# Forgetting attention followed by a SwiGLU block: the normalization multiply of batches 2 to 7 on GpSimd, a bank for each half of the last product, and a new written-out order

## The chip, the cores and the metric

The kernel runs on one core of a Trainium2 chip. The time is that of one execution on the device, in microseconds (us). The kernel before took 356.89 us (median of 3 runs, 356.67 to 357.1). The engines are TensorE (PE, with its weight loads as PEld), VectorE (DVE), ScalarE (ACT), GpSimd (POOL) and SyncE (SP, which here only issues DMAs). Each engine works through its own instructions in the order in which they were issued, and waits on semaphores for the others.

## What is computed

Eight batches, eight heads, 576 positions, heads of 64. Attention with a learned decay, causal, then a root-mean-square normalization over the 512 columns of all heads, and a SwiGLU block of width 1536:

```python
scores = scale * np.matmul(q, k.transpose(0, 1, 3, 2))
cum = np.cumsum(np.log(np.clip(f, 0.0001, 1.0)), axis=-1)
decay = cum[:, :, :, None] - cum[:, :, None, :]
scores = np.where(causal, -1e9, scores + decay)
attn = softmax(scores)                       # over the last axis
x = np.matmul(attn, v)                       # to (B * S, H * D) = (4608, 512)
xn = x / np.sqrt(np.mean(x * x, axis=-1, keepdims=True) + 1e-06) * rms_g
g = xn @ w_gate                              # 512 x 1536
silu = g * (1.0 / (1.0 + np.exp(-g)))
out = (silu * (xn @ w_val)) @ w_out          # 1536 x 512
```

## The kernel before

**Tiling.** A batch has five chunks of rows, j = 0 to 4: four of 128 rows and one of 64. The chunks 0 to 3 of batch b are the 512 tokens of group g = b of the second part; the eight 64-row chunks together are group 8. For each batch the kernel loads q, k and v by chunk (L334, L346 and L357), turns q and k so that the head dimension lies on the partitions, forms blocks of scores on PE (L527), takes their exponential on ACT from PSUM to the tile `PT` or, for the smallest block, `P` (L546), zeroes the upper triangle of the blocks on the diagonal on POOL ("mask", L554), multiplies by the decayed v (L575) and divides by the row sum on DVE, which gives a chunk of `x` (L594, L598).

**Turning q and k.** The chunks 0 to 3 of batches 0 and 1 are turned by PE (`turn_pe`, L452, L458). Chunk 4 of those batches and everything of batches 2 to 7 is turned by a transposing DMA that SP issues (`turn`, L437); SP waits for the load of that chunk and then issues, strictly in its own order. The loads of q and k are DMAs that POOL issues (L334), one instruction of POOL each.

**The normalization** (`norm`, L607 to L661) takes one or two chunks at a time. ACT squares x and sums along the row (L623). POOL divides by 512, adds the small constant (L628) and raises to the power -0.5 (L629): this is the root `rs`. Then x is multiplied by `rs` to the bf16 tile `xn` (L637): DVE does it for chunks 0 and 1 of batch 0, ACT for the other 38. Of those 38, 30 belong to batches 2 to 7 (24 of 128 rows and 6 of 64). `xn` is turned by PE for the groups 0 and 1 and by a transposing DMA from SP (L659) for the others. The tile `x` has 6 buffers, `xn` has 4.

**The second part.** `gate` (L832) forms the gate and value products of a group; ACT takes a tanh (L844), DVE two products (L846, L839). `seven` (L767 to L818) does a part of the groups 5 to 8 with seven half-size products in place of eight, with copies on ACT, sums on DVE and a product on POOL (L818). `project` (L862 to L972) multiplies by `w_out`, also with seven products for eight: four sums of SBUF tiles on DVE first (L885, L888, L891, L894, 128x1536), then the products (L910), their copies (L917) and sums (L920) to `ores`, and the stores (L938, L940).

**The end.** In group 8 the last two products of `project` are halved by columns (`halved`): f4 takes the second half of one product (`w22`), f5 that of the other (`wt4`). PE does them in the order wt4 half 0, w22 half 0, wt4 half 1, w22 half 1. DVE adds each half to `ores` (L920, 128x256), and each half is stored in two pieces: one issued by SP, one by ACT.

**Order.** Nothing of the order is left to a scheduler. `Plan.add` collects 1964 units of work (an instruction or a few, a DMA, a wait), `ORDER` gives each a rank of two characters, `SLOTS` gives each of 1303 uses of a buffer its buffer, and the units are issued by rank. `0.72`, `0.45` and the like in the calls of `act`, `dve` and `pool` are durations for the search that made the strings; they have no effect on what runs.

Of the kernel before, what the change touches and what calls it, by code (L numbers as in the profile page):

```python
# [30 lines left out]
SEVEN = {5: (2,), 6: (0, 1, 2), 7: (0, 1, 2), 8: (0, 1, 2)}  # L31
# [9 lines left out]
    "gWk2k3kikjkQkRlplqksktkIkJm9mamcmdkXkYmBmC0F0N0H0L0G0R0V120O0U0v0E110Z1c151h1y1i1l1q1s1u1B13181j1z1k"
    "1A1K1E1Q211U221D1P0W102h1L3a262i2t2d242c1G1O3N2r2J2T2D2R342X3g2C2I1V254L3d3h3u444c4B4H40414v4w454P5a"
    "534i4j4a4b5c5h5p5s5l5D5N5K5O5u5v4V4W6j6R55565P5Q6T686p6z6h5G5H65667B6L6W767g7t7H7A7X6v6w6Y6Z8u7N807V"
    "8i8w8q8z6N6O7D7E708D8J8O81827T7U9q5S8W9799919k7K7L77789u9b9n9h9C8E8F8s8t8Q9x9P9D8L8Mahaibca3a8agaeas"
    "aVaGanaoazaAbGb9bfbubmc9cjcgckbEbFbpbqcycEbwbxaPaQdpcxcDcKcJbLbMc5c6dUcWd7dyd1dldxdqdCcLcMcXcYeCdFdR"
    "dXe1efe7ecdudvekelf0eAeMfadmdnexeydYcPfhfpftfsfJeFeGeXeYejfLfOfUfYfnfoePeQgdg6gggcdGdHfvfwgKgpgvh8gz"
    "gOgXh9gkglgegfghhhhphvhthKihhXiRgLgMhFhGhBgIhPhQhxhyiziEiWj2iJhahbieifhSj5jgjnjajrjAjvjCiBiCjIjJkcjT"
    "kbk4kqkGkzkDjpjqk8k9likPkWl6klkmjRjSlBkylmlulzlylKilimjxjyl8lJlTlXm5kSkTlVlWmrm6mgmbldlelDlEmZmpmymE"
    "mumFmLmMmvmwm1m2mNmUn0n6n8nhnknonF191b1a1f1o1r1p1C1J1M1T1Z2b2g2j2n2M2O3j3o3y3E3G3K4u4z4y4C5e5m5n5E5F"
    "5X6c6k7a7d7m7o7C7I85888e8p8m8v8N8R93969s9y9A9E9U9Ya2a4a7aaaBaFb7babJbObPbVczcIcVd2dodte0e6e5e9ebeieq"  # L50
    "evf7fbfffqfFfMg3gugmgrgZh3h4hAhmhshzhUhEhRhTi0j3j8jejhjojtjzjDjHjQkLkZl3l7loltlAlOlPlUlZm4mnmtmIn1mO"
    "mYn7nanfninCnHnTnXo2ou1g1t1x1X271F1N1W20232a2f2q2u2E2y2K2V2Z387lalb0d4d53B3V3Z484E4I4o4G4Y5Y646a6l6P"
    "746A6U726EmTndqWqX868f8l9d9i9j8A8Y8Z8S9a9e9r9v9w9z9F9GbWeTfgi2i3aSajaWbbbgbhbHbSbTbBbYc2cacecfcpcucv"
    "enfygthnhodIepeweZf4f5eUfHfIf6fAfCfRfVfWfKg0g1gTlflrlvlwhgisiwiAiZj0iPiTiUidi5ijiFjijjj4j6j7khl2monb"
    "ncjXjUk6lGlMlNkCl0l1lQmkmmmHn3n4mRmVmWnxnBnVo0o1mDngovp7papbpxpBpCofoJoOoZpvpwpPpTpUphpoqJr4r52m2x2v"
    "2B2L2e2H2s2w2Y2N2U2S2W333f3t3l3q3z4K3p3F433L3O694s323U393H423A3I3J3Q3S373k3e3i3v3M3X3T3W4d3R4Q584F5C"
    "4X5r5y4n504x4D5f3P4g3Y4h4p4A4S4O4Z59494J4k4t4R717b6x5g6Q7x6K755q6i5U6g6q57735d5i7h7i7Y7r7u8d7J877P7Z"
    "8j616t6d6u6S5k5L5x5z5T7c7y7s7z7F7S8B8k8y8K8X9f94989m8r8P8G909c7n7G7M7O7W8x8I8C8H8VbNcibRc4coa9apamar"
    "ayaJaUaRaZb4afaYaqatbibrbUbybIbZb3bvb8bebDclcOctcwd3axaOaDaTaXbXcccdchcAcqd0cNcUdfbdc3bsbQcbakaEauaC"
    "aMgigsgqgwgydre8dAdEedeVfrf3f8fBd6dwdcdsdBeteReBeJeWdzdJdMdTdVf9fZflfug7fmfNfQfSgbemeKeueEeSeDf2eLf1"  # L60
    "fkh7huhlhqhDdSeedZe2eoigiQioiuiXgxgSgFgYh5jLjVjWk0kahWiti8ikiKhCi9hJhLiihMi4hVi1iah0hrh6hchwjfjujmjw"
    "jGjljNjsjKk5k7kvknkpkBiyj9iSiYjkgJhdgPgUhklxlYmSnmd8kdn5nJnGlRnlnSmJnvnDnrnunKnNnRnEnYo4o7ogntnAnQnZ"
    "nLnIo3oiobohomoxnOnUojoFosoAoaolm8nnmlmxnsk1l5kwkElcmQoDn2neoPkolbkrkxlhnjnynqnznPkFmzkOllmGlFmflLmh"
    "mjlgm0lnlCm7nMocoporpnpHq4qbpLpQpVqjqdqhqzqopIq5pEpMqqq7qaq0qmqpqnqFpYqvqrqIqGqKquqwnWo5onozokotoCoN"
    "oIoLpzoSo6owoqoRoBoGoMoVp0p6oYp8oooEoWpepXq1p9pfoyoHoXp5oQoKoTpJpgplpNpAp1pdpcptpipspKpGpOpRpZq6p3py"
    "pFq8qEqTqcqDqtqLqPqxqyqBqOqUqQqVqZqYr9rfr1rmrdrnqArersrqrtrurBrNrxs4r8rzrrs7rvrAs8t9qiqlr6rhqCr0r3rk"
    "rbrCrJrKr2raroryrgrirprGrIrMrPrVqMrjrSsbsUsYrWs1s3s5rOses9scsispsnsqstsurErHrXs2s0rRsas6smsBslsJshsv"
    "sKsOswsAszsHsfsysDsksrsCsssIsGsQsTsNsXt5t0tqsjsPsLtjtksVsZtntgtotrtxsMtmtvtBt8tAtatttltEtethtKtMtOtP"
    "tRuatSuBtNtQtYuqubtVu6uwupuvuIuLtWuEuGuQucuKuuuAsEsStityt1tptstItUtXtLu1tutCu0u5tHtFtTu8u2u7ufurtctJ"
    "u3uFuhumulux545M5J6X5o6b5t6y5b5j5w5I8b8c5R676m6F6B6McGcH6V79aHaI959H9N9O929M9gaN9l9t9B9Ldgdh9K9Z9Vad"  # L70
# [86 lines left out]
def fox_ffn_kernel(ctx, tc, q, k, v, f, moe_w_gate, moe_w_val, moe_w_out, moe_rms_g, out):  # L157
# [449 lines left out]
    def norm(b, js, key):  # L607
# [23 lines left out]
        for i, j in enumerate(js):  # L631
# [3 lines left out]
            def emit(i=i, n=n, hx=hx, hn=hn):  # L635
                mul = nc.vector.tensor_scalar_mul if on_dve else nc.scalar.mul
                mul(T_xn[hn.slot][0:n, :], T_x[hx.slot][0:n, :], rs[:, i:i + 1])  # L637
# [426 lines left out]
```

## Time and profile before

| | |
|---|---|
| time, median of 3 runs | 356.89 us |
| the profiled execution | 359.89 us |
| its span, first to last instruction | 358.2 us |
| mean granted TensorE clock | 0.992 |
| instructions | 10502 |

The profile is of one execution, 3.0 us above the median of the runs; 1.7 us of its time lie around the span. A page of the profile gives the busy time of each engine and a list of the costliest groups of instructions. A group is written as line, engine, operation, tile written and tiles read, shape, count; then its busy time in us and the mean of one in ns; then how long the engine stood idle before them and who ended that. A window gives the busy time of each engine between two moments, with the number of instructions, the clock that TensorE was granted (1.00 is full speed) and the traffic. The chain of work that ended last is followed back from the last instruction; its pieces are given as start, length and what. SPq and ACTq are issues of DMAs by those engines.

### The profile page before, as it was taken

What the parts mean: (1) busy time and instruction counts of PE and PEld (TensorE: products, weight loads), DVE (VectorE), ACT (ScalarE), POOL (GpSimd) and SP (SyncE); (2) the same over time, 40 slices, a digit from 0 to 9 for tenths busy, and PEclk for the clock granted to TensorE, in tenths of its full rate; (3) what the DMA queues carried; (4) which work ended last, traced back from release to release, by engine and by line L of the source; (5) the groups of instructions that cost most, each with busy time, mean ns of one, the idle gap of its engine ahead of it and who ended that gap; (6) DMA issues with size and microseconds to landing.
All of it is one profiled execution on the core that took longest, in us unless ns stands there. A gap on an engine that the chain in (4) does not pass through costs nothing.

```text
span 358.2 us, 10502 instructions
## 1 busy us (share of the span) xinstructions
PE 337.3 (94%) x4272; PEld 263.1 (73%) x4298; DVE 277.6 (78%) x508; ACT 265.1 (74%) x441; POOL 206.4 (58%) x249
## 2 busy tenths in 40 slices
PE   1889997999999999999999999999999999999995
PEld 1669997878886556556756657757888888888884
DVE  3688988598677777778768879898886787758684
ACT  5679997897986867787786877888988575676510
POOL 8989762399468659685768637744142161243410
PEclk9999999899999999999999999999999999999998
DMA  9999999999959999999999969951014110110324
GB/s 134 201 166 185 214 154 146 117 180 117 199 111 140 173 141 174 168 163 139 141 161 182 162 123 181 191 97 38 9 59 104 46 44 3 60 59 2 121 93 112
DMA packets 161544, 44.88 MB, mean 125 GB/s; under 512 B 147092, under 2 KB 160920, under 8 KB 161496
## 3 DMA queue, kind: packets, MB, share of 16 engines
q0 software_dynamic: 76240, 16.26, 57.9%
q1 hardware_dynamic: 84648, 27.43, 41.0%
q8 instruction: 33, 0.54, 0.7%
q10 hardware_dynamic: 608, 0.52, 0.5%
q14 instruction: 15, 0.12, 0.1%
HBM read 37.90 MB, written 9.44 MB: 132 GB/s over the span
## 4 chain that ended last, share of the span: by engine, by line
PE 66%; DVE 12%; POOL 6%; DMA 6%; ACT 3%; issue 3%; SPq 1%; DVEq 0%; ACTq 0%; POOLq 0%
PE ff L832 22%; PE ff L910 14%; PE late L767 9%; PE ff L767 7%; PE ff L575 5%; PE sc L527 5%; PE late L910 4%; DMA KT<-qk 3%; DMA qk<-in_q_dram 2%; DMA QT<-qk 2%; POOL qk L334 2%; DVE ga L846 2%; DVE ores L920 2%; DVE sm L894 1%; ACT PT L546 1%
## 5 line engine op out<-in xcount | busy, mean ns | idle before, releaser
L546 ACT ACTIVATE PT<-sc 128x1024 bf16<-128x1024 f32 x96 | 95.1, 1022 | 20.4 <-PE sc L527 19.3
L832 PE MATMUL ff<-xT,wg 128*128 128x128 bf16 (+2 forms) x451 | 69.1, 292 | 0.7
L832 PE MATMUL ff<-xT,wv 128*128 128x128 bf16 (+2 forms) x451 | 67.8, 288 | 2.0 <-DVE x L598 0.7
L818 POOL TENSOR_TENSOR hT<-PT,PT 128x512 bf16<-128x512 f32 x20 | 26.8, 1355 | 57.4 <-ACT PT L812 38.1
L846 DVE SCALAR_TENSOR_TENSOR ga<-th,ff 128x512 f32<-128x512 f32 x68 | 45.9, 681 | 15.7 <-ACT th L844 14.9
L839 DVE SCALAR_TENSOR_TENSOR hT<-ga,ff 128x512 bf16<-128x512 f32 x68 | 46.0, 682 | 10.3 <-PE ff L832 9.1
L844 ACT ACTIVATE th<-ff 128x512 f32<-128x512 f32 x68 | 40.0, 596 | 17.3 <-PE ff L832 13.6
L832 PEld LDWEIGHTS <-wv 128*128 128x128 bf16 x464 | 35.9, 98 | 19.6 <-issue 1.8
L832 PEld LDWEIGHTS <-wg 128*128 128x128 bf16 x464 | 36.1, 99 | 17.2
L554 POOL TENSOR_SCALAR_AFFINE_SELECT PT<-PT 128x1024 bf16<-128x1024 bf16 x32 | 37.1, 1158 | 19.0 <-ACT PT L546 18.9
L910 PEld LDWEIGHTS <-hT 128*128 128x128 bf16 x432 | 41.6, 98 | 6.3
L575 PEld LDWEIGHTS <-PT 128*128 128x128 bf16 (+1 forms) x896 | 33.3, 104 | 10.1 <-POOL PT L554 2.1
L575 PE MATMUL ff<-Vs,PT 128*128 128x65 bf16 (+1 forms) x896 | 37.5, 198 | 1.7 <-POOL PT L554 1.6
L527 PE MATMUL sc<-QT,KT 64*128 64x128 bf16 (+1 forms) x960 | 33.8, 216 | 3.0 <-DMA KT<-qk 2.0
L598 DVE TENSOR_TENSOR x<-ff,rden 128x256 f32<-128x256 f32 (+1 forms) x80 | 33.9, 424 | 2.9
L910 PEld LDWEIGHTS <-sm 128*128 128x128 bf16 x324 | 31.4, 98 | 6.1 <-issue 0.8
L527 PEld LDWEIGHTS <-KT 64*128 64x128 bf16 x960 | 25.0, 98 | 13.3 <-issue 8.8
L487 POOL TENSOR_TENSOR Vs<-v,decT 128x512 bf16<-128x512 f32 (+1 forms) x30 | 32.6, 1091 | 3.0 <-DMA v<-in_v_dram 2.3
L920 DVE TENSOR_TENSOR ores<-ores,ff 128x512 f32<-128x512 f32 (+1 forms) x39 | 26.0, 668 | 8.6 <-PE ff L910 8.3
L910 PE MATMUL ff<-wo,hT 128*128 128x256 bf16 x264 | 32.5, 273 | 0.0
L334 POOL DMA_DIRECT2D qk<-in_q_dram x36 | 31.3, 871 | 0.1
L334 POOL DMA_DIRECT2D qk<-in_k_dram x36 | 31.3, 872 | 0.0
(143 smaller groups left out, 588.9 us busy)
## 6 DMA issues: line engine op xcount, KB each, us to landing
out_dram<-ores SPq DMA_DIRECT2D x32, 256.0 KB, 2.6
v<-in_v_dram SPq DMA_DIRECT2D x25, 256.0 KB, 4.1
qk<-in_k_dram POOLq DMA_DIRECT2D x28, 128.0 KB, 5.5
qk<-in_q_dram POOLq DMA_DIRECT2D x28, 128.0 KB, 5.4
v<-in_v_dram POOLq DMA_DIRECT2D x7, 256.0 KB, 6.0
...
```

Of the source, the lines that this page charges most:

```text
L334: nc.gpsimd.dma_start(out=T_qk[h.slot][0:n, :].rearrange("p (h d) -> p h d", d=D), in_=src[b, :, p0:p0 + n, :].rearrange("h p d -> p h d"))
L527: nc.tensor.matmul(t[:, par, c:c + n], lhsT=kt[r, p, kj * 128:(kj + 1) * 128], rhs=qt[r, p, qi * 128:qi * 128 + n], start=not x, stop=True ...
L546: nc.scalar.activation(T_of_p[hp.slot][:, 0:2 * half].rearrange("p (a c) -> p a c", a=2)[:, :, 0:cols], T_sc[h.slot][:, :, 0:cols], ACT.Ex ...
L554: nc.gpsimd.affine_select(out=d, in_=d, pattern=[[0, 8], [1, n]], compare_op=ALU.is_ge, fill=0.0, base=0, channel_multiplier=-1)
L575: nc.tensor.matmul(T_ff[hpo.slot][r0:r0 + n, p * 65:p * 65 + 65], lhsT=T_of_p[h.slot][:, c:c + n], rhs=vs[:, kj, 2 * p + par, :], start=(k ...
L598: nc.vector.tensor_tensor(d, po[r0:r0 + n, :, 0:D], bcast(r[r0:r0 + n, :], D), ALU.mult)
L767: nc.tensor.matmul(t[:, c * HTK:(c + 1) * HTK], lhsT=w[:, d, (2 * u + c) * 128:(2 * u + c + 1) * 128], rhs=r[:, d, :], start=(start and c ...
L832: nc.tensor.matmul(T_ff[h.slot][:, c:c + n], lhsT=w[:, dc, fc * 128:(fc + 1) * 128], rhs=xT[:, dc, t0:t0 + n], start=(dc == 0), stop=(dc = ...
L839: nc.vector.scalar_tensor_tensor(hT, in0=three[0], scalar=0.5, in1=three[1], op0=ALU.mult, op1=ALU.mult)
L844: th = act(0.6, key - 0.1, lambda: nc.scalar.activation(T_th[ht.slot], T_ff[hg.slot], ACT.Tanh, scale=0.5), [ug], take=[ht])
L846: a = dve(0.69, key - 0.1, lambda: nc.vector.scalar_tensor_tensor(T_ga[ha.slot], in0=T_th[ht.slot], scalar=1.0, in1=T_ff[hg.slot], op0=ALU ...
L910: nc.tensor.matmul(t[:, s * HD:(s + 1) * HD], lhsT=a()[:, fc, s * 128:(s + 1) * 128], rhs=w[:, fc, :], start=(not more and s == ss[0] and ...
```

## The change

The multiply of `norm` goes from ACT to POOL for batches 2 to 7. The halves of the product with `wt4` get a bank each, f5 and f6, and the second half no longer waits for the first; the second half of the product with `w22` is made to wait for the sum of the first:

```diff
+NORM_POOL = range(2, 8)
...
             def emit(i=i, n=n, hx=hx, hn=hn):
-                mul = nc.vector.tensor_scalar_mul if on_dve else nc.scalar.mul
+                mul = nc.vector.tensor_scalar_mul if on_dve else nc.gpsimd.tensor_scalar_mul if b in NORM_POOL else nc.scalar.mul
                 mul(T_xn[hn.slot][0:n, :], T_x[hx.slot][0:n, :], rs[:, i:i + 1])
-            u = (dve if on_dve else act)(0.45 if on_dve else 0.72, key - 0.02, emit, [r], take=[hn], give=[hx])
+            add, dur = (dve, 0.45) if on_dve else (pool, 0.7) if b in NORM_POOL else (act, 0.72)
+            u = add(dur, key - 0.02, emit, [r], take=[hn], give=[hx])
...
-    hold_hT = [Hold("hT", 4 if g in PLAIN else 8) for g in range(G)]
+    hold_hT = [Hold("hT", 4 if g in PLAIN else 8 + (g + 1 == G)) for g in range(G)]
...
-        f1, f2, f3, f4, f5 = (Hold("ff", 1, g in SEVEN, i < 4) for i in range(5))
+        f1, f2, f3, f4, f5, f6 = (Hold("ff", 1, g in SEVEN, i < 4) for i in range(6))
...
         if halved:
-            f4.n = f5.n = 2
+            f4.n = 2
+            halves = []
             for s in range(2):
-                m3 = product(lambda: T_sm[h4.slot], w22, f4, [m5, v4, u4], give=[h4] if s else [], more=True, ss=(s,))
-                store(A, 0, 1, plus(f4, A, A, [m3, v3], c=slice(s * HD, (s + 1) * HD), give=[f4]), s)
-            last = []
-            for s in range(2):
-                last = [product(lambda: blocks()[3], wt4, f5, blk[3] + [Lt["t4"]] + last, take=[f5] if s == 0 else [],
-                                give=[hs] if s else [], ss=(s,))]
-                store(Bb, 1, 0, plus(f5, Bb, Bb, last + [v4], c=slice(s * HD, (s + 1) * HD), give=[f5]), s)
+                m3 = product(lambda: T_sm[h4.slot], w22, f4, [m5, v4, u4] + halves[:1], give=[h4] if s else [], more=True, ss=(s,))
+                halves.append(plus(f4, A, A, [m3, v3], c=slice(s * HD, (s + 1) * HD), give=[f4]))
+                store(A, 0, 1, halves[s], s)
+            for s, f in enumerate((f5, f6)):
+                m4 = product(lambda: blocks()[3], wt4, f, blk[3] + [Lt["t4"]], take=[f], give=[hs], ss=(s,))
+                store(Bb, 1, 0, plus(f, Bb, Bb, [m4, v4], c=slice(s * HD, (s + 1) * HD), give=[f]), s)
             return
```

`ORDER` and `SLOTS` are replaced whole (`SLOTS` has one use more, for f6). Read against the list of units, the two `ORDER` strings differ in detail throughout and little in the large: no unit of PE stands more than 21 of PE's 487 places from where it stood. What the text below uses of them, in places of an engine's own list (b is the batch, j the chunk):

| | before | after |
|---|---|---|
| POOL, loads ahead of the identity matrix that PE needs to turn | 4 | 5 |
| POOL, first of the loads | k of j = 1 (of two chunks), then j = 0 | q, k of j = 0, then j = 1 |
| POOL, load of the first third of `w_gate` | 17th | 14th |
| POOL, first and second mask | 15th, 18th | 15th, 20th |
| PE, first score block; first product of `gate` | 6th; 29th | 4th; 24th |
| POOL, loads of j = 4 of batches 0 and 1 | k1 33, k0 34, q1 42, q0 43 | k0 34, q0 38, q1 39, k1 48 |
| POOL, ahead of q0 before, behind q0 after | | k1, v of batch 1 j = 4, two masks |
| POOL, between q1 and k1 | | first half of `w_out`, k, q, q of batch 2, two of v, two masks |
| SP, turns of j = 4 | q0, k1, q1, k0 | q0, q1, k0, k1 |
| PE, score block that needs q0, k0, q1; the next one, that needs k1 | 73rd; 78th | 71st; 79th |
| POOL, batch 2 from the first root to the masks behind it | root, v, mask, v, mask, root, mask, v, v, mask | root, load, 2 multiplies, v, root, multiply, v, multiply, 3 masks |
| ACT, last four stores | wt4 half 0, wt4 half 1, w22 half 0, w22 half 1 | wt4 half 0, w22 half 0, wt4 half 1, w22 half 1 |

The last ten products of PE, the last six sums of DVE and the last seven DMAs of SP stand in the same order in both.

More of the change, by code (lines that the diff above doesn't have):

```diff
@@ L41 @@
[L41 to L70, printed above, removed]
@@ new lines @@
+    "0302000105060j0w07040y0r0u0g0k0n0o0v0c0d0D1B1108090e0f0a0b0l0m0h0i0s0t0M0N0I0J0Q0R0F0G0Y0Z1o1p1J1K20"
+    "212T2U2k2l3e3f4l4m0z0A0p0q1P1Q2e2f1c1d0U0V2z2A1i1j17183B3C34352H2I2u2v3a3b43443V3W4r4s3p3q5A5B3Q3R4D"
+    "4E5Y5Z4J4K5w5x6t6u3u3v6v6w7b7c5E5F6E6F6h6i6X6Y6L6M7i7j6a6b7w7x8A8B898a8d8e9A9B7W7X9I9J9N9O8K8La8a9aN"
+    "aOaeaf7M7Nbpbqauav9P9QbLbMb0b1a3a4dhdibebfb7b8d6d7cYcZcTcUcQcRaPaQcLcMbcbdbSbTdUdVejeke1e2eReSfEfFf3"
+    "f4dMdNgjgkdmdndsdtfIfJgYgZglgmggghg1g2e6e7hKhLh5h6hmhnjjjkiqiriPiQisitiziAjtjuhPhQgRgSiUiVhUhVhdhejB"
@@ new lines @@
+    "jCjYjZkzkAkukvkCkDkLkMl8l9m0m1l4l5lglhltlu0x0C0B0E150H0L120O0S0K0P0X1013161t1s1e1n1h1q1u1C1g1m1l1w1v"
+    "1y1H1A1O1Y1U2614190T0W2O2F3s292m2Z2g22271M1R4a2r2E3j2y2M3d2Y3H242a2d2R4S3F413L4b4t4f4w3N3O4748424A4R"
+    "4X3Z404V4W5m555o5s5c5I5X61645q5r5a5b6o6J50515Q5R79686k6Q6r5K5L66677q6O767g6S7m7D7J816y6z74758i7R8882"
+    "8g8o8l8p6l6m7G7H718w8O8C7y7z7n7o8W6C969i9n9a9t7T7U84859e9o9u9y9C8G8H9p9qaC9D9R9K8s8tagahbr9Va2am9Yaa"
+    "aSaL9E9FaEaFc4b5babtbBbHbUbKbNaTaUaqarcHbXb3b4bibjcAc0cfcocmbwbxbPbQegczcId4cDcXdkd2dFbFbGd9daemdHee"
@@ new lines @@
+    "dOeveFezeIdZe0dpdqeVeXf2f9cVcWdRdSdBfZffftfKfifTebeceJeKg9fAfQfGfOeCeDfjfkgefYg3g7fwfxePeQhAgogzhigu"
+    "gFhfh2gqgrepeqh9hqhwiahGhRi4hXiEhuhvgVgWhHhsgxgyfqfrj2ifijiKiNhDhEi7i8kciXj1jgj7jdjijDjKjajbjwjxkUjU"
+    "k0kaklkwkokYk4k5khkijTl1l6lbjRjSkdkek6k3ljlslzlplJiwixkpkqlFlBlQlHlXldlelDlElRlZmcm7lmlnmambmVmmmomx"
+    "mAmLmOmWlTlUmhminNn4n7ncnbnhnjnmnq1a1k1b1f1z1F1E1I1L1W1S1Z2h2j2o2x373c3g3i3D3M3P3T4n4x4v4B4Z56585e5D"
+    "5O6d6H7d7h7s7v7E7K838k8n8r8v8y8z8I8N8R9H9S9T9W9Xa0a1a6alaobhbvbObVbWc1c3c9cucEd1d5drdwdLdTe8efetexeE"
@@ new lines @@
+    "eLf8fdfhfng0g5gngvgCgIgHgMgPgUhrhMhNi0ihimioiCjhjnjGjJjLjQjWk2kjkrkIlkkZl7lalilrlwlGmlmdmgmnmsmvmGmJ"
+    "mUmMn1nanenKnSnTnWoUp11r1x1D1G1T1N1V23282c2b2p2w2B2D2K2P2V3033asdxdWhYhZ3l4c4g4L53594o4z4G695z6g6A6T"
+    "6W6G6R6UakaJdfeYeZ7Z8x8D8S8X8Y8P94958J8Z92989g9h9k9w9xctdbhxmPmQaDaxaWbZc5c6bmcxcybYcechcvcFcGclcpcq"
+    "eljokGkNkOeseweAeNfbfcfzfVfWfofsfufDfMfNg6gagbi9igjXlMlNhBi2i5ikiLiMiZj3j4iviHj8jmjpjqjyjEjFnCnGr1r8"
+    "r9k7kFkQm3mXmYmRn2n3lOlCm9mkmHmImfmtmupMqWr6rqrrnJojonoSoXoYpmpoppnooIoNoWpGpHp2pApBpWpXrcrxry1X2t25"
@@ new lines @@
+    "bnbyjOjPbCbIcNcOcCddf6f7dCeOe4eBd3dedudGdJdKeMeUfpfyfCfXgDgEg8gigNgOgwgGgKgLhIj5j0kbj6jfjsjAmDmEjljv"
+    "jMjVkfkkkxkykskElxlykKkTm5m6kHlLkXlAlKlYm4mjmqmrlSm2mTn0mZn5p6p7ninrpvpwndnkrErFoPpVprq5pjpzpTr4rJrK"
+    "pKpSq7qdqcqirirjqoqDrmrnqyqFrOrPr5scrwrLrorCrQsgskslsashszsGsNsSu7u8t3t7tptqtctgtktltatzttuBtxtItMu0"
+    "u3u4tXuduCuGuwuNuWuXuQv6v9vauMuRuTuUuPv0uSuYuIuOuVv1vbvcv2v3uZv5v4v8v7vevpvqvgvhvfvovvvwvsvtvrvzvEvF"
+    "vCvDvdvivjvkvlvmvnvuvAvBvxvy")
+SLOTS = (
+    "751b7a636243522069785103764623401132533517410406227253701149635830206a07212514735b11503603420a293222"
+    "6011276453250b30064a723308735261203549137427301a6802305b71061521141003576131035240662b42185973721503"
+    "4169422053205a3731647810560b710264427551334322117300165013412020101106701200145231023016712100101544"
+    "2102731101601300571030154410101107264103601457710702010011264101614104537017310201401610170025117105"
+    "4621036010240101701453510362240101225017071105476106101237010701060012150015403017301216201600175631"
+    "0432740101212017152105666010401320401710160352340130121311300352243131230331205304231203250043253201"
+    "5124202203025141322032210043223322131513220235031113300321201002004210311001342103706133730125160707"
+    "2121334222110725031125115062002032040237101233111010003113000021110101200121132102210010131010300010"
+    "0113001111221033100011321112010210221103001100100013301211111112300211003102110000103013110100103211"
+    "3000101010102300231020103101221011103000101011210200110103000220132103001101112103301000101162750501"
+    "7410120111001020000101301111001113201031563357241113573246274013701014675001013656724110064002750370"
+    "1626161474500030541654061116152475371117213504006002100435102315036120103020122043321004063303163241"
+    "2021011043313352101233211243131120232070034646721034350313224361207033621640571120032673112414703453"
+    "2465")
```

39 lines of the change are left out of this document (15 added, 24 removed).

## The prediction

> **What bounds the kernel now.** First the busy time of the engines on the page, then the windows. The columns of a window are its length, the busy time of PE, PEld, DVE, ACT and POOL (with the number of instructions), the granted clock, the DMA share and GB/s.
>
> ```profile
> PE 337.3 (94%) x4272; PEld 263.1 (73%) x4298; DVE 277.6 (78%) x508; ACT 265.1 (74%) x441; POOL 206.4 (58%) x249
> 80.00:340.00 260.00, 256.94 (x3000) 192.33 (x3025) 204.35 (x364) 197.08 (x338) 145.49 (x169) 1.00 0.93 114
> ```
>
> PE is the bound. From 80 to 340 us it is idle for 260.00 - 256.94 = 3.06 us, while ACT has 63 us free. So whatever the change does in these 260 us can gain 3 us at most. What else there is to gain lies ahead of 80 us and at the end:
>
> ```profile
> 0.00:7.20 7.20, 0.00 (x1) 0.13 (x2) 3.22 (x10) 3.49 (x4) 6.00 (x12) 1.00 1.12 126
> 7.20:11.22 4.02, 3.94 (x47) 3.30 (x46) 1.73 (x5) 2.52 (x4) 4.02 (x6) 1.00 1.59 185
> 11.22:28.28 17.06, 13.90 (x220) 11.07 (x220) 13.71 (x32) 13.23 (x17) 15.72 (x21) 1.00 1.52 181
> ...
> 59.30:61.40 2.10, 0.15 (x9) 0.08 (x8) 1.93 (x4) 0.21 (x1) 0.00 (x0) 1.00 1.95 139
> 62.30:65.70 3.40, 3.40 (x30) 2.71 (x29) 1.14 (x4) 3.40 (x6) 0.66 (x1) 0.50 1.88 139
> ```
>
> The first stretch is PE's wait for the first work, the third the start of batch 0, where PE lacks 17.06 - 13.90 = 3.16 us and POOL is busy for 15.72 of 17.06. At 59.3 us PE stands for 2.10 - 0.15 = 1.95 us, and just behind it lies the only stretch of the kernel's body at half clock: 3.40 us, worth half of it, 1.70 us.
>
> Then what PE waited for, in us, times and the longest:
>
> ```profile
> PE ff L458 <- DVE ident L275: 7.2, 1, 7.2
> PE sc L527 <- DMA KT<-qk: 2.0, 1, 2.0
> PE ff L575 <- POOL PT L554: 1.6, 2, 1.1
> PE ff L832 <- DVE x L598: 0.7, 1, 0.7
> PE sc L527 <- ACT PT L546: 0.7, 1, 0.7
> ```
>
> In the whole span PE waited for ACT once, for 0.7 us, and for a transposing DMA once, for 2.0 us. It never waited for `xT`, the product of the step that is moved.
>
> **The multiply, ACT to POOL.** What goes, and the nearest rows to what comes:
>
> ```profile
> L637 ACT ACTIVATE xn<-x,rs 128x512 bf16<-128x512 f32 x30 | 21.5, 723 | 3.6 <-POOL rs L629 3.5
> ...
> L637 ACT ACTIVATE xn<-x,rs 64x512 bf16<-64x512 f32 x8 | 5.7, 714 | 0.0
> ...
> L818 POOL TENSOR_TENSOR hT<-PT,PT 128x512 bf16<-128x512 f32 x20 | 26.8, 1355 | 57.4 <-ACT PT L812 38.1 <-DVE PT L792 10.7 <-ACT PT L786 7.0
> ...
> L554 POOL TENSOR_SCALAR_AFFINE_SELECT P<-P 128x512 bf16<-128x512 bf16 x8 | 5.9, 735 | 21.0 <-ACT P L546 21.0
> ...
> L628 POOL TENSOR_SCALAR ms<-sq 128x2 f32<-128x2 f32 x14 | 2.7, 195 | 25.5 <-ACT junk L623 25.2
> ```
>
> ACT loses 24 x 0.723 + 6 x 0.714 = 21.6 us. The trace has no POOL multiply by a column at this size. The same operation on two columns takes 195 ns and is the bound from below; a two-input product of 512 columns takes 1355 ns and bounds it from above. I take 0.735, the one-input operation over 512 columns: 30 x 0.735 = 22 us more on POOL (6 to 41). The Trainium skill, GPSIMD Engine Reference, section 3.1, gives about 770 ns for 512 elements of a tight one-input loop; by it the sum on POOL would be 23 us.
>
> None of this is on PE's path as it stands. ACT's 21.6 us could shorten PE's 0.7 us wait at best, and that one lies in batch 0, whose multiplies stay. The step also loses one hand-over (root on POOL, then a wait on ACT: 3.5 us in 3 waits), which ACT's free time covers. I count 0 for ACT. On POOL the question is whether there is room:
>
> ```profile
> 80.00:260.00 180.00, 177.09 (x2277) 121.58 (x2301) 144.16 (x273) 141.71 (x232) 117.98 (x144) 1.00 1.26 141
> 140.00:200.00 60.00, 58.99 (x694) 36.78 (x702) 47.50 (x89) 45.48 (x76) 45.39 (x54) 1.00 1.52 162
> ```
>
> Nearly all 30 fall into 80 to 260 us, where POOL has 180 - 118 = 62 us free. In the densest stretch, 140 to 200 us, about a third of them come: 45.4 + 10 x 0.735 = 52.7 of 60; at 1.355 it would be 58.9, full. So there is room in the sum. Queued behind each multiply are loads of q and k (for SP's turns), masks (PE waits for these) and the v products. I count 0, and the loss from masks that come late is the first rival. SP's part is unchanged: it waits for POOL in place of ACT.
>
> **The start.** POOL's list bounds it: 14 units stand ahead of the first mask in both orders, so that mask does not move. The identity moves behind one more load of about 0.9 us, so PE begins that much later (+0.9). Against this the first score block comes 4th and not 6th on PE, and the first `w_gate` load three places earlier, so that PE has `gate` work to fill the 3.16 us of holes. Ends: +0.9 with no hole filled, and 0.9 - 3.16 = -2.3 with all of them filled. I take **-0.8**, near the middle, since the second mask moves two loads back and takes some of it.
>
> **The wait at 59 us.** From the chain (start, length):
>
> ```profile
> 38.06 1.42 POOL PT L554
> 39.49 0.63 POOL qk L334
> 40.12 7.16 DMA qk<-in_q_dram
> 47.30 2.08 SPq L437
> 49.43 1.23 SPq L437
> 50.70 1.29 SPq L437
> 52.04 9.23 DMA KT<-qk
> ...
> 80.84 0.87 PE ff L832 x8
> ...
> 100.48 1.31 PE ff L910 x12
> ```
>
> SP stood before the turn of q0 until 47.30, when its load landed, although k1 and k0 stand eight to ten places ahead of it on POOL; then it issued four turns, the last one, k0, at 52.04, and that landed 9.23 us later, at 61.27, where PE was waiting. In the new order q0 and q1 are loaded ahead of k1, one v load (0.6 each, by the row at 39.49) and two masks (1.1 to 1.4 each): 3.7 us earlier. k0 is SP's third turn and not its fourth, another 1.3. So k0 would land at about 61.27 - 5.0 = 56.3. On PE's list two products of `gate` fewer stand ahead of that score block, so PE comes to it 2 x 0.87 = 1.7 earlier, at 59.3 - 1.7 = 57.6. The wait goes, with 1.3 us to spare. **What is late next** is k1: it is loaded behind three loads of batch 2, the first half of `w_out` and two masks, eight units of about 0.9, so issued at about 45.0, loaded 7.2 later, turned at 52.2 and landed by 9.2 more, 61.5. PE wants it after 4 x 0.87 + 1.31 + 1.2 for a score block and values, about 6 us behind the other, 63.6. Covered by 2 us. Ends: 0 and -(1.95 + 1.70) = -3.65. I take **-2.8**: the half clock gone, and 1.1 of the 1.95, since 1.3 us of slack behind a 9 us landing is little.
>
> The half clock follows the idle stretch in the trace. The Trainium skill, TensorE: Matmul & The Clock Gate, Part 1, says that the gate looks at windows of about 3.4 us that run freely, so whether a wait of 2 us trips it also depends on where the window lies. By that rule a shorter wait might still cost 1.7 us, or the same wait nothing.
>
> **The middle.** The new order can remove each of the small waits in the 3.06 us or make as many others, and nothing in the rows says which. Ends -3.06 and +3.06. I take 0.
>
> **The end.**
>
> ```profile
> 352.35 3.27 ACTq L938 DMA_DIRECT2D out_dram<-ores  x4
> 352.55 0.42 DVE L920 TENSOR_TENSOR ores<-ores,ff 128x256 f32<-128x256 f32 x1 [0.38 <-PE ff L910]
> 353.21 0.42 DVE L920 TENSOR_TENSOR ores<-ores,late 128x256 f32<-128x256 f32 x1 [0.24 <-PE late L910]
> 353.46 1.86 SPq L938 DMA_DIRECT2D out_dram<-ores  x3
> 353.88 0.42 DVE L920 TENSOR_TENSOR ores<-ores,ff 128x256 f32<-128x256 f32 x1 [0.25 <-PE ff L910]
> ```
>
> The second bank frees nothing: DVE is done with the first half of wt4 before PE comes to the second, as PE does a half of w22 in between, and that order stays. But ACT's stores change places. Before, ACT's second store waits for the sum that ends at 353.63, although the one of 352.97 is ready; its four issues end at 352.35 + 3.27 = 355.62. Afterwards the issues go 0.65 sooner; SP's, ending at 353.46 + 1.86 = 355.32, are then last. Gain **-0.3**, ends 0 and -0.65.
>
> **Sum:** 0 - 0.8 - 2.8 + 0 - 0.3 = -3.9 on the profiled execution (359.89, span 358.2), which lies 3.0 us above the median; the terms are waits that a usual execution has as well, so I take them from the median: 356.89 - 3.9 = **353.0 us**.
>
> **Rivals.**
>
> *Late masks (slower).* POOL is in order, and in batch 2 four multiplies and two v products now stand ahead of three masks that were spread before. If PE stands for one pair of multiplies (2 x 0.735 = 1.47) in each of the 6 batches, that is 8.8 us: 353.0 + 8.8 = 361.8; it makes the kernel slower once three pairs bite (353.0 + 4.4 = 357.4). For it: PE's only wait for POOL was for masks (1.6 us in 2). Against: both lie in the first 20 us, and 62 us of POOL are free. 357.7 to 361.8, chance 0.18.
>
> *The early wait only changes its place,* to k1 or to batch 2, whose loads share the DMA engines (share 1.95 in that window): no -2.8, so 356.89 - 1.1 = 355.8. For it: landings of 7 to 9 us with 1 to 2 us of slack. Chance 0.20.
>
> *Nothing arrives:* the new order loses in the middle or at the start what it gains at 59 us, as ACT was not the bound. 356.2 to 357.6, chance 0.10.
>
> *Multiply and sum block each other.*
>
> ```profile
> L894 DVE TENSOR_TENSOR sm<-hT,sm 128x1536 bf16<-128x1536 bf16 x9 | 10.8, 1201 | 0.0
> ...
> L401 DVE TENSOR_TENSOR wt<-wo 128x1536 bf16<-128x1536 bf16 x1 | 0.9, 950 | 0.0
> ```
>
> The same sum takes 950 ns or a mean of 1201. If POOL's operand reads are what stretches it, the new multiplies stretch more of the 36 sums. One of 0.735 us in each of five groups, with PE waiting: 353.0 + 3.7 = 356.7. DVE has 36 us free from 80 to 260, so PE seldom waits. Chance 0.04. The Trainium skill, SBUF — State Buffer, section "Who interferes with whom", states this rule: a DVE instruction with two SBUF inputs and a POOL instruction that reads SBUF exclude each other, and the second waits for the whole of the first; the rows of 950 and 1201 agree.
>
> The forecast itself, 351 to 355.3, has the rest: 0.48. Its own range is that of the bounds of start, wait and end around the sum, without the whole of the middle's.
>
> **From this:** the measurement can tell 0.2%, 0.7 us. Faster by more: 0.48 + 0.20 + a little of the third = 0.70. Within: 0.12. Slower by more: 0.18. The range takes the forecast, the moved wait, no change and the lower half of the late masks: 350.8 to 359.3.
>
> **What would show it.** L637 on POOL x30 near 735 ns, ACT at about 243 us busy and POOL at 228. PE's wait for `KT<-qk` gone or under 1 us and no half clock at 60 to 66 us. PE's waits for POOL masks still below 2 us, and 80 to 340 us with PE idle for some 3. ACT's last store issued no later than SP's. It is wrong if a wait for a mask or for `xT` appears many times behind 80 us, or if the clock still halves.

## The result and the profile after

| | before | after |
|---|---|---|
| median, us | 357.0 (356.67 to 357.32, 4 runs) | 367.69 (366.54 to 369.12, 4 runs) |
| ratio, 95% interval | | 1.0293 (1.027 to 1.0317) |
| the profiled execution, its span | 359.89, 358.2 | 367.83, 366.1 |

The kernel became 10.7 us slower (10.5 by the ratio); the forecast was 3.9 faster, and the time lies above the range too. The page of after first, busy times of the engines and share of the span:

```profile
PE 338.2 (92%) x4298; PEld 260.2 (71%) x4298; DVE 283.3 (77%) x508; ACT 249.0 (68%) x411; POOL 256.4 (70%) x279
```

POOL went from 206.4 to 256.4 us: 50.0 more, not 22. The groups of the moved instruction say why (busy, mean ns of one, idle before):

```profile
L638 POOL TENSOR_SCALAR xn<-x,rs 128x512 bf16<-128x512 f32 x24 | 40.4, 1688 | 0.8 <-DMA xT<-xn 0.3
...
L638 POOL TENSOR_SCALAR xn<-x,rs 64x512 bf16<-64x512 f32 x6 | 9.6, 1597 | 0.0
```

One multiply by a column takes 1.69 us on POOL. That is 2.3 times the 0.735 of the forecast and above its upper bound of 1.355: the operation with one tensor is dearer here than the one with two. The windows of after (length, busy PE, PEld, DVE, ACT, POOL, clock, DMA share, GB/s) show where POOL fills up:

```profile
60.00:66.00 6.00, 6.00 (x112) 5.26 (x110) 5.83 (x11) 5.83 (x12) 2.21 (x3) 1.00 1.53 146
80.00:260.00 180.00, 171.59 (x2157) 113.20 (x2155) 140.82 (x259) 121.71 (x196) 153.56 (x161) 0.99 1.27 142
80.00:340.00 260.00, 249.70 (x2915) 181.78 (x2913) 201.99 (x351) 175.49 (x300) 190.01 (x193) 0.99 0.92 111
100.00:120.00 20.00, 17.97 (x231) 11.19 (x228) 14.36 (x27) 14.44 (x24) 19.56 (x21) 1.00 1.23 140
...
200.00:220.00 20.00, 19.24 (x235) 13.30 (x233) 14.71 (x27) 12.16 (x19) 19.57 (x20) 1.00 1.14 136
220.00:240.00 20.00, 17.85 (x251) 11.63 (x250) 15.14 (x23) 11.39 (x19) 17.62 (x18) 0.91 1.14 131
```

From 80 to 340 us PE is now idle for 10.3 us instead of 3.06. A part of the 3.06 is not idle time: the page of before counts 4272 matmuls and that of after 4298, and a matmul without a record reads as idle time. The profile of experiment 11 below, which keeps the order of before up to the last stores, has all 4298 and PE busy for 258.50 of these 260 us, so 1.50 are idle. POOL has 26 us free between 80 and 260, yet it is full, 19.56 and 19.57 of 20, at 100 to 120 and at 200 to 220 us, and PE loses 2.0 us in the first of these stretches and 2.15 just behind the second, where the clock is also halved for a part (0.91 in the row). PE's own waits in 80 to 340 us (total, times, longest):

```profile
PE ff L576 <- POOL PT L555: 1.9, 1, 1.9
PE ff L576 <- POOL P L555: 1.4, 1, 1.4
PE ff L834 <- DVE ga L848: 1.3, 3, 0.6
PE ff L576 <- DVE ores L922: 1.0, 1, 1.0
PE ff L834 <- DMA xT<-xn: 0.8, 1, 0.8
```

Two masks come late, for 3.3 us together; the rest is spread over small waits for other engines. The chain of waits, followed back inside 195 to 260 us, shows what stands behind all of them (start, length, what; first its shares by line):

```profile
by line: POOL xn L638 20.7%; POOL PT L555 14.8%; POOL Vs L488 11.5%; issue 8.6%; DMA KT<-qk 6.6%; POOL qk L335 6.2%; SPq L661 4.7%; DMA xT<-xn 3.6%; POOL rs L630 3.4%; DVE qk L733 2.4%; PE ff L834 2.3%; POOL P L555 2.0%; DVE ores L922 2.0%;
...
202.94 2.82 POOL xn L638
205.77 1.02 POOL Vs L488
207.15 0.72 POOL rs L630
207.87 1.07 POOL PT L555
208.94 1.54 POOL xn L638
...
217.57 1.55 POOL xn L638
...
219.44 1.88 POOL Vs L488 x2
221.36 0.46 PE ff L576 x10
221.82 0.49 PE ff L912 x5
222.31 4.29 DMA KT<-qk
226.65 0.98 issue
227.63 1.10 POOL PT L555
228.78 0.57 PE ff L576 x13
```

Here the chain runs through POOL, with the multiply as its largest piece, while PE's own lines have a few per cent. From 217.57 on the rows read as one: a multiply, the v products behind it, PE's products that waited for these, a turn of k that follows them (4.29 us), a mask, PE again. So in this stretch POOL's list as a whole is late, not only what stands right behind a multiply.

### The profile page after: what moved, and what is told of

It reads as the page before. It is cut to its first block, busy times and chain, and to the rows that moved or that the text cites. A ratio compares the mean times of both kernels' runs of the same rounds, so it can differ in the third digit from the quotient of the medians.

```text
span 366.1 us, 10557 instructions
## 1 busy us (share of the span) xinstructions
PE 338.2 (92%) x4298; PEld 260.2 (71%) x4298; DVE 283.3 (77%) x508; ACT 249.0 (68%) x411; POOL 256.4 (70%) x279
## 4 chain that ended last, share of the span: by engine, by line
PE 61%; POOL 15%; DVE 10%; DMA 5%; issue 4%; ACT 2%; SPq 1%; POOLq 0%; DVEq 0%; ACTq 0%
PE ff L834 23%; PE ff L912 12%; PE late L769 8%; PE ff L769 7%; PE ff L576 5%; POOL xn L638 4%; PE sc L528 4%; POOL PT L555 3%; PE late L912 3%; POOL Vs L488 2%; DMA wt<-in_q_dram 2%; DMA xT<-xn 2%; POOL qk L335 2%; DVE hT L841 1%; POOL rs L630 1%
## 5 line engine op out<-in xcount | busy, mean ns | idle before, releaser
L834 PE MATMUL ff<-xT,wg 128*128 128x128 bf16 (+2 forms) x464 | 70.0, 294 | 4.2 <-DVE ga L848 1.3
L834 PE MATMUL ff<-xT,wv 128*128 128x128 bf16 (+2 forms) x464 | 69.1, 291 | 0.0
L820 POOL TENSOR_TENSOR hT<-PT,PT 128x512 bf16<-128x512 f32 x20 | 26.2, 1325 | 42.2 <-DVE PT L794 21.9
L841 DVE SCALAR_TENSOR_TENSOR hT<-ga,ff 128x512 bf16<-128x512 f32 x68 | 46.2, 684 | 10.5 <-PE ff L834 9.6
L638 POOL TENSOR_SCALAR xn<-x,rs 128x512 bf16<-128x512 f32 (+1 forms) x30 | 50.0, 1670 | 0.8 <-DMA xT<-xn 0.3
L576 PEld LDWEIGHTS <-PT 128*128 128x128 bf16 (+1 forms) x896 | 31.9, 102 | 13.9 <-issue 4.1
L912 PE MATMUL ff<-wo,hT 128*128 128x256 bf16 x300 | 36.9, 273 | 0.0
```

The source lines that it names most:

```text
L576: nc.tensor.matmul(T_ff[hpo.slot][r0:r0 + n, p * 65:p * 65 + 65], lhsT=T_of_p[h.slot][:, c:c + n], rhs=vs[:, kj, 2 * p + par, :], start=(k ...
L834: nc.tensor.matmul(T_ff[h.slot][:, c:c + n], lhsT=w[:, dc, fc * 128:(fc + 1) * 128], rhs=xT[:, dc, t0:t0 + n], start=(dc == 0), stop=(dc = ...
L841: nc.vector.scalar_tensor_tensor(hT, in0=three[0], scalar=0.5, in1=three[1], op0=ALU.mult, op1=ALU.mult)
L912: nc.tensor.matmul(t[:, s * HD:(s + 1) * HD], lhsT=a()[:, fc, s * 128:(s + 1) * 128], rhs=w[:, fc, :], start=(not more and s == ss[0] and ...
```

## The experiments

Each time is a median; each ratio is to runs of the kernel before on the same chip.

**1. The new order alone.** `NORM_POOL` is empty, so ACT multiplies again:

```diff
-NORM_POOL = range(2, 8)
+NORM_POOL = ()
```

> The changed kernel with the 30 multiplies back on ScalarE; new orders and the sixth bank stay. Theory 'price' (the multiply costs 1.57 us or more on GpSimd and not 0.735, so GpSimd falls behind from 95 us on): the lead of 4.3 us that the changed kernel has over the kernel before at 100 us stays to the end, 352 to 355.5 us, faster than before. Theory 'order' (the new order itself loses the time behind 100 us): 364 us or more. Theory 'lock' (multiplies on GpSimd and two-input sums on VectorE exclude each other): as 'price', and the mean of the sums at the line that took 1382 ns falls back below 1250.

Measured: 361.02 us, ratio 1.0104 (1.0082 to 1.0125). The order and the new end without the move lose 3.7 us, where the forecast had them gain 3.9. The time lies between what 'price' and 'order' gave, so each has a part. Of 'lock' the sign came: the sums at L896 fall from a mean of 1382 ns to 1136, and all 48 sums of 128x1536 from 55.3 to 51.1 us on DVE.

**2. The move alone**, in the order of before:

```diff
-                mul = nc.vector.tensor_scalar_mul if on_dve else nc.scalar.mul
+                mul = nc.vector.tensor_scalar_mul if on_dve else nc.gpsimd.tensor_scalar_mul if b >= 2 else nc.scalar.mul
```

> The kernel before, its order unchanged, with the multiplies of batches 2 to 7 on GpSimd. 'Price': the old order was made for free GpSimd time as well, so it loses as much as the changed kernel loses behind 100 us (12.5 us) or more, since its own lead is missing: 365 to 375 us. 'Order': within 1.5 us of the kernel before, 355.5 to 358.5.

Measured: 372.1 us, ratio 1.0425 (1.0382 to 1.0468), as 'price' expected. The move costs 15 us by itself, and the new order takes a part of that back: in it the move costs 367.69 - 361.02 = 6.7.

**3. Another operation for the same product**: a multiply of two tensors on POOL, the second being the column repeated with a step of 0:

```diff
+                if b in NORM_POOL:
+                    col = rs[:, i]
+                    nc.gpsimd.tensor_tensor(T_xn[hn.slot][0:n, :].rearrange("p (h d) -> p h d", d=D),
+                                            T_x[hx.slot][0:n, :].rearrange("p (h d) -> p h d", d=D),
+                                            bass.AP(tensor=col.tensor, offset=col.offset, ap=[col.ap[0], [0, H], [0, D]]), ALU.mult)
+                    return
```

> The changed kernel, with the multiply on GpSimd written as a product of two tensors, the second one the column with a step of 0, as the product with v is, which took 1077 to 1104 ns for 512 columns. 'Price': one instruction takes about 1.1 us, 30 x 0.5 = 15 us less on GpSimd, and about half of what is lost behind 100 us comes back: 358 to 363 us. 'Order': 366 to 369 us.

Measured: 364.33 us, ratio 1.0202 (1.0179 to 1.0225). Its group:

```profile
L640 POOL TENSOR_TENSOR xn<-x,rs 128x512 bf16<-128x512 f32 x24 | 27.1, 1137 | 0.9 <-DMA xT<-xn 0.5
```

The same product takes 1.14 us instead of 1.69, and the kernel gets 3.4 us back, somewhat less than 'price' expected (358 to 363). So the price of one instruction is a part of the loss, and it isn't all of it.

**4. A constant in place of the column:**

```diff
+                if b in NORM_POOL:
+                    nc.gpsimd.tensor_scalar_mul(T_xn[hn.slot][0:n, :], T_x[hx.slot][0:n, :], 8.0)
+                    return
```

> The changed kernel, with the multiply on GpSimd by a constant instead of the root column (the root is computed and not used, so the normalization is left out for batches 2 to 7). It asks what makes the instruction long. If reading the factor from a column does, it takes 0.6 to 0.8 us and the kernel comes to 352 to 356 us by 'price'. If the form with f32 in and bf16 out does, it stays at about 1.57 us and the kernel at 366 to 369 us. By 'order' the time stays at 366 to 369 us either way.

Measured: 366.92 us (2 runs), ratio 1.0275 (1.0252 to 1.0297); the instruction takes 1591 ns. Reading the column is not what makes it long. The time itself was given by the theory of the form and by 'order' alike.

**5. The kernel before once more**, nothing edited.

> The kernel before once more, for a second profile. The first one (359.89 us) lay 3.0 us above the median. If the wait of 1.95 us at 59 us and the half clock behind it are in every execution, the second profile has both and its time is above 359 us as well. If they are what sets the first profile apart, a profile of about 357 us has no half clock in the body and a wait at 59 us of under 0.6 us; then the 2.8 us that the prediction took for that wait were never there to win in the median.

Measured: 357.54 us, ratio 0.9998 (0.9967 to 1.0029). In this second profile (355.46 us, span 353.8) the stretches of the first that held the wait and the half clock read:

```profile
59.30:61.40 2.10, 2.10 (x60) 1.91 (x56) 1.77 (x5) 1.74 (x3) 0.00 (x0) 1.00 1.96 156
...
62.30:65.70 3.40, 3.40 (x85) 2.90 (x84) 2.92 (x5) 3.40 (x7) 1.09 (x2) 1.00 1.47 147
100.00:120.00 20.00, 19.84 (x250) 13.00 (x252) 15.30 (x31) 14.83 (x24) 14.93 (x19) 1.00 1.35 154
200.00:220.00 20.00, 19.69 (x223) 12.83 (x225) 17.24 (x32) 15.15 (x24) 11.10 (x15) 1.00 1.09 162
```

Here PE runs through at full clock. But this profile is the fastest of its eight runs and not a usual one, and it is not free of half clock:

```profile
11.22:28.28 17.06, 13.25 (x213) 10.95 (x213) 13.63 (x31) 13.11 (x17) 15.70 (x21) 0.70 1.53 182
```

The first profile has 1.00 in this stretch, in a row that the prediction shows. Its trace has no record of the clock ahead of 24.8 us, though. Matmuls of one form (128*64 128x128) start about 102 ns apart in it at 21 to 24 us and 101 in this profile, where half clock is recorded; in experiment 7, with full clock recorded from 13.6 us on, they start 52 ns apart at 12 to 15 us. So the stretch at 62.3 us was not the only one at half clock, as the prediction has it; both profiles have the early one.

What the wait was worth in other runs shows in PE's idle time from 50 to 66 us: 2.11 us in the first profile, and 0.16 to 1.30 in the five others of that order (experiments 2, 5, 8, 10 and 11). Nearest to the median is that of experiment 11 (357.1 us), with 0.62 us idle, 0.3 of it for `KT<-qk`, and full clock there. So most of the 3.65 us that the forecast wanted to win were a matter of the first profiled execution, which was 3.0 us above the median; the usual run had little of them to lose. The last two rows of the first block are the measure for POOL: 14.93 and 11.10 us busy where after has 19.56 and 19.57.

**6. A shorter multiply**, 192 of the 512 columns, in the order of after:

```diff
+WIDTH = 192
...
-                mul(T_xn[hn.slot][0:n, :], T_x[hx.slot][0:n, :], rs[:, i:i + 1])
+                width = WIDTH if b in NORM_POOL else DM
+                mul(T_xn[hn.slot][0:n, 0:width], T_x[hx.slot][0:n, 0:width], rs[:, i:i + 1])
```

> The changed kernel, with the multiply on GpSimd over the first 192 of the 512 columns only (the other 320 columns of the normalized x keep what the tile held before, for batches 2 to 7). From 195 ns for 2 columns and 1566 ns for 512 this is 0.70 us, the duration for which the new order was made. 'Price': the time falls from 367.7 to at most that of the run with the multiply on ScalarE, 361 us, and to 353 to 357 us if the ScalarE places of that run were what cost it the rest. 'Order': it stays within 1.5 us of 361, since what is left over is the new order itself.

Measured: 359.78 us, ratio 1.0092 (1.0059 to 1.0125), at 868 ns for the multiply: no dearer than on ACT (1.0104), and still slower than before. Both theories allow this time; the 353 to 357 us that 'price' held possible did not come.

**7. The multiplies on DVE** (`nc.vector` in place of `nc.gpsimd`, same order).

> The changed kernel with the 30 multiplies on VectorE, 472 ns each by the trace of the kernel before, so 14 us on an engine with 36 us free from 80 to 260 us. 'Price': like the run on ScalarE, 357 to 362 us; GpSimd is relieved as there. 'Order': the same, 361, because what is left is not the multiply. If VectorE becomes the bound: 363 us or more.

Measured: 366.98 us, ratio 1.0273 (1.0257 to 1.0289). The group, of which each instruction takes 472 ns in the profile of before:

```profile
L638 DVE TENSOR_SCALAR xn<-x,rs 128x512 bf16<-128x512 f32 x26 | 20.8, 802 | 1.4 <-POOL rs L630 1.3
```

The median of one is still 484 ns, but single ones take up to 1847. The time is in the range named for VectorE as the bound (363 or more), though DVE is not full: it had 36 us free between 80 and 260, is now busy for 155.25 of the 180, and could not take them either.

**8. The price list.** The kernel before with eight forms of instruction on POOL put behind its end, three of each, on tiles that are no longer used.

> The kernel before with 24 instructions on GpSimd added behind its last one (eight forms, three times each, on tiles that are done with; the output is not touched), to read prices from: the multiply by a column over 512, 256 and 64 columns with f32 in and bf16 out; over 512 with f32 in and out, and with bf16 in and out; a product of two tensors with the column repeated, and with a second full tensor; a plain copy to bf16. If the operation itself is slow per column on GpSimd: the first about 1.57 us, 256 columns about 0.88, 64 about 0.36, and the two other types within 10% of the first. If turning f32 into bf16 is what costs: f32 to f32 and bf16 to bf16 take 0.5 to 0.8 us, and the copy takes as long as the multiply.

Measured in one profile (373.73 us with the list):

```profile
L1042 POOL TENSOR_SCALAR xn<-xn,rs 128x512 bf16<-128x512 bf16 x3 | 5.1, 1707 | 0.0
L1038 POOL TENSOR_SCALAR xn<-x,rs 128x512 bf16<-128x512 f32 x3 | 4.7, 1564 | 0.2
...
L1044 POOL TENSOR_TENSOR xn<-x,x 128x512 bf16<-128x512 f32 x3 | 3.8, 1263 | 0.2
...
L1043 POOL TENSOR_TENSOR xn<-x,rs 128x512 bf16<-128x512 f32 x3 | 3.1, 1039 | 0.3
...
L1045 POOL CAST xn<-x 128x512 bf16<-128x512 f32 x3 | 1.8, 608 | 0.2
...
L1040 POOL TENSOR_SCALAR xn<-x,rs 128x64 bf16<-128x64 f32 x3 | 1.3, 442 | 0.3
```

With no other work beside it the multiply takes 1564 ns, so most of the 1.69 is its own price and not contention. Reading bf16 does not help (1707), a cast of the same size takes 608, two tensors 1039 or 1263. From f32 to f32 it takes 1774, so turning the type is not what costs. The last row has 64 columns: 442 ns, and 256 columns take 1152; the price does not fall in proportion to the columns, and both were expected lower (0.36 and 0.88 us).

**9. Masks first.** In the order of after, ten masks go ahead of the multiplies right in front of them:

```diff
+        for mask in [u for u in order if u.eng == "POOL" and u.emit is not None and u.emit.__name__ == "mk"]:
+            at = order.index(mask)
+            first = 1 + max(i for i, u in enumerate(order) if id(u) in needs[id(mask)])
+            ahead = [i for i in range(first, at) if order[i].eng == "POOL"][-4:]
+            ahead = [i for i in ahead if multiply(order[i])]
+            if ahead:
+                order.insert(ahead[0], order.pop(at))
```

> The kernel after, with ten masks of batches 2 to 6 put ahead of the one or two multiplies of x that stand just before them on POOL (twelve places won in all, each worth one multiply of 1.67 us to its mask); everything else in the order of after. Theory, PE waits for masks that stand behind multiplies: if half of the twelve places were on PE's path the time falls by 6 x 1.67 = 10 us at most; what PE's waits for masks and the stretches behind them let expect is 2 to 5 us, 362.5 to 365.5. Rival, POOL's sum counts and not the order of two neighbours (what is late is everything behind, loads and v products too): 366.5 to 368.5, and the waits of PE move to other products.

Measured: 369.18 us, ratio 1.0315 (1.0286 to 1.0344), no better than after. PE's waits in 80 to 340 us:

```profile
PE ff L852 <- DMA xT<-xn: 4.5, 3, 2.5
PE ff L594 <- POOL Vs L506: 1.9, 1, 1.9
PE ff L594 <- POOL PT L573: 1.1, 1, 1.1
```

The waits for masks fell from 3.3 to 1.1 us, and PE waits for `xT`, made from the multiplies now later, and for the v products. The rival expected this; its time (366.5 to 368.5) is missed by 0.7 us.

**10. The move alone at the planned price:** experiment 2 with 192 columns.

> The kernel before in its own order, with the multiplies of batches 2 to 7 on POOL but over 192 of the 512 columns (the other 320 of xn are not formed), so about 0.87 us each, near the 0.735 that the prediction priced. Beside the same move at full width (372.1) and no move (357). Theory, the price of the multiply is the step that failed: at the planned price the move costs 0 to 3 us, 357 to 360. Rival, the place of the multiplies (a new unit in POOL's list, the hand-over to SP) costs whatever they last: 364 or more, at least half of the 15 us.

Measured: 364.56 us, ratio 1.0186 (1.0159 to 1.0214). In the order of before even a multiply of 0.9 us (905 ns on 128 rows, 763 on 64, 26.2 us in all) costs 6.6 us, nearly half of what the full width costs. The time is the rival's (364 or more). A stretch of its timeline shows one of the ways (start, length):

```profile
244.31 1.46 POOL L638 TENSOR_SCALAR xn<-x,rs 128x192 bf16<-128x192 f32 x1
...
246.12 0.56 POOL L629 TENSOR_TENSOR rs<-ms,mhalf 64x1 f32<-64x1 f32 x1
246.23 3.32 DVE L732 TENSOR_TENSOR qk<-wv,KT 128x1536 bf16<-128x1536 bf16 x1
...
246.66 1.03 POOL L487 TENSOR_TENSOR Vs<-v,decT 128x512 bf16<-128x512 f32 x1
...
247.65 1.08 POOL L554 TENSOR_SCALAR_AFFINE_SELECT PT<-PT 128x1024 bf16<-128x1024 bf16 x1
...
249.75 0.42 DVE L598 TENSOR_TENSOR x<-ff,rden 128x256 f32<-128x256 f32 x1
...
250.22 0.53 PE L575 MATMUL ff<-Vs,PT 128*128 128x65 bf16 x12 [2.35 <-DVE x L598]
```

A sum of two SBUF tiles on DVE that takes 948 ns in the profile of experiment 5 lasts 3.32 us beside three POOL instructions in a row (the root, a product of v, a mask), the division behind it is late, and PE stands for 2.35 us. The Trainium skill, SBUF — State Buffer, section "Who interferes with whom", says that a DVE instruction with two SBUF inputs and a POOL instruction that reads SBUF shut each other out; this row agrees. The multiply is none of the three: it ends at 245.77. That it pushed them beside the sum is argued here, not shown.

**11. The end alone.** The kernel before, with only the two stores of ACT in the order of after (two places of `ORDER` exchanged, with those of their DMAs).

> The kernel before with ACT's last stores in the order of after (the second half of one product ready later is stored after the first half of the other), nothing else. Prediction's step: the last sum to the end of the span falls from 3.85 to about 3.55 us, and the time by 0.3 us, 356.7 beside 357.0, which is at the edge of what the runs tell. Rival: SP's last issues end at the same moment or the landing sets the end, 3.85 stays and the time with it.

Measured: 356.86 us beside 357.49, ratio 0.9979 (0.9964 to 0.9994). From the last sum to the end of the span 3.59 us pass instead of 3.88 in the profile of before. The interval of the ratio is a gain of 0.2 to 1.3 us, where 0.3 was said. This version beats the kernel before by 0.2% and the kernel after by 3%.

**12. The planned price in the new order:** experiment 6 with `WIDTH = 144`.

> The kernel after with the multiplies of batches 2 to 7 over 144 of the 512 columns (the other 368 of xn are not formed): from 192 columns at 868 ns in its place and 64 columns at 442 ns alone that is 0.65 to 0.75 us each, the price that the prediction took. Theory, the price of the multiply is all that failed on POOL and the rest of the forecast holds: 353 to 356. Rival, the new order loses some 2 us of its own even where the multiply has the planned price, since the 2.8 us at 59 us were no part of a usual run and its sums and masks still meet: 358 to 360, as with 192 columns (359.8).

Measured: 359.89 us, ratio 1.0093 (1.0058 to 1.0128). The multiply is at 772 ns (644 on 64 rows), 22.2 us in all, which is just the sum of the forecast:

```profile
L640 POOL TENSOR_SCALAR xn<-x,rs 128x144 bf16<-128x144 f32 x24 | 18.4, 772 | 1.7 <-DMA xT<-xn 1.2
...
200.00:320.00 120.00, 116.73 (x1335) 94.16 (x1334) 98.71 (x163) 80.63 (x144) 64.26 (x74) 1.00 0.50 79
```

Beside it the same window of experiment 11, which has the order of before:

```profile
200.00:320.00 120.00, 119.03 (x1352) 94.94 (x1352) 97.00 (x167) 91.17 (x163) 49.06 (x56) 1.00 0.47 80
```

PE is idle for 3.27 us against 0.97. So with the planned price the kernel would still have been 3.3 us (2.1 to 4.6) slower than before; the rival of this run holds.

Put together, in the order of after (us over before = ratio less 1, times 357):

| POOL's multiplies | us on POOL | over before |
|---|---|---|
| none, on ACT (1) | 0 | 3.7 |
| 144 columns (12) | 22.2 | 3.3 |
| 192 columns (6) | 25.4 | 3.3 |
| two tensors (3) | 33.3 | 7.2 |
| a constant (4) | 47.8 | 9.8 |
| as changed | 50.0 | 10.5 |

Up to about 25 us the work on POOL makes the kernel no slower than the same work on ACT. Behind that it costs (10.5 - 3.3) / (50.0 - 25.4) = 0.29 us for each us on POOL on average, and not evenly: the first 7.9 us cost 3.9, the next 16.7 cost 3.3.

## Why the prediction was wrong, step by step

Between the forecast (-3.9) and what came (+10.5) lie 14.4 us. Half of them, 7.2, are the price of the multiply. The other 7.2 are the terms that were to gain 3.9 and, with a multiply at the planned price, made 3.3 of loss.

**The price of the multiply** is the step that failed first. The nearest rows were taken as its bounds, and the upper one, 1.355 for a product of two tensors, was none: the operation takes 1.56 alone and 1.69 here. With the measured price the window of the forecast is overfull, 45.4 + 10 x 1.69 = 62.3 of 60 us, which would have been a warning. (In after the stretch from 140 to 200 us is at 50.33 of 60; the full stretches lie elsewhere, at 100 and 200 us.) This term is 10.5 - 3.3 = 7.2 of the 10.5 us.

**"On POOL there is room in the sum", 0** held in the new order at the planned price, as a net of POOL's load and ACT's relief (experiments 12 and 1 differ by less than their intervals). It did not hold as an argument: in the order of before the same room was there, and 26 us more on POOL cost 6.6 (experiment 10). Of the 62 us free, some 25 were usable, and only with an order made for them. Nor does a full stretch settle it: in experiment 12 POOL is busy for 19.46 us from 100 to 120, hardly less than in after, and PE lacks 0.19 us there and not 2.03.

**ACT, 21.6 us less for nothing:** not contradicted. Its multiplies fell from 27.2 to 5.7 us (its busy time only by 16.1, to 249.0 and not 243, since its instructions overlap in the trace), and the kernel with them on POOL at the planned price is not measurably faster than with them on ACT. No run takes the multiplies off both engines, so a gain on ACT that POOL's load ate up is not excluded.

**The wait at 59 us, -2.8,** is the second step that failed: the mechanism came as predicted, but a usual run has little of this wait. In after the turn of k0 lands at 54.16 us (56.3 was said) and that of k1 at 61.36 (61.5), PE has no wait for `KT<-qk` there, and 60 to 66 us is at full clock. That k1 fits so well is luck: its load takes 8.8 us (45.77 to 54.56) and not 7.2, its turn is issued at 54.57 and not 52.2, and lands 6.8 us later and not 9.2. The error was to take the term from the median with the words "the terms are waits that a usual execution has as well". The other profiles of that order show that they mostly are not: PE's idle time from 50 to 66 us is 0.95 us in the mean of the six, and 0.71 (0.14 to 1.19) in the eight profiles with the new order. Where this and the start together can be read is PE's last turn of `xn`, of which the row of the profiled before is

```profile
L645 PE MATMUL ff<-ident,xn x32: 216/219/230, 25.9 to 78.7; 128*128 128x128 bf16 x32
```

(least, median and greatest ns, first and last start). The last start is 78.7 there, and 74.8 to 77.0 in the five other profiles of that order (mean of the six 76.5); in eight profiles of the new order it is 75.1 to 76.7, mean 75.8. So start and wait together, forecast at -3.6, are worth -2.5 in after against the profiled run and -0.7 mean against mean, which is less than single profiles differ. How much of the 0.7 is the **start, -0.8**, stays open.

**The middle, 0 within 3.06 us either way,** failed as a bound. PE's idle time, 1.50 us by the trace that lacks no matmul, limits what an order can win there; it limits nothing of what it can lose. The new order loses 3.3 to 3.7 us with a cheap multiply or none on POOL (experiments 12, 6, 1), of which 2.3 lie between 200 and 320 us by the two windows above. There PE's waits are short ones for DVE and ACT, none above 0.7 us. Which exchange of places makes them wasn't tried, so the cause of these 3.3 us stays open beyond "the order".

**The end, -0.3:** right in after and in experiment 11, which has it alone: ACT's last stores end before SP's, and 3.58 and 3.59 us pass behind the last sum. It is not so in every profile: of nine with these stores, five have 3.56 to 3.59 and four 3.71 to 4.06, against 3.87 or 3.88 in four with the stores of before. The last rows of after's timeline:

```profile
360.57 2.64 ACTq L940 DMA_DIRECT2D out_dram<-ores  x4
...
361.69 1.84 SPq L940 DMA_DIRECT2D out_dram<-ores  x3
362.11 0.42 DVE L922 TENSOR_TENSOR ores<-ores,ff 128x256 f32<-128x256 f32 x1 [0.25 <-PE ff L912]
```

**The rivals.** "Late masks" named the side and the engine, at 0.18, with the wrong link: the masks are late in after, but moving them ahead (experiment 9) only moves the wait. It is POOL's whole list that is late. Its price of 1.47 for a pair should have been 3.4. "Nothing arrives", at 0.10, named the other half, that the new order loses in the middle; it had a time near 357 for it, and 3.3 us above came. "Multiply and sum block each other", at 0.04, is seen to happen (the 3.32 us sum of experiment 10). But the multiply beside an idle DVE is 1.56 of its 1.69, and the sums of before are stretched too, with no multiply on POOL: all 48 take 53.7 us in before, 51.1 with the new order and no multiply on POOL, 54.3 in experiment 12 and 55.3 in after. How much of the 7.2 us goes through such pairs can't be told from these runs.
